# One core, sigmoid attention into routed experts into SwiGLU: table copies on VectorE, ranks first, three block buffers

## The chip, the cores and the metric

The kernel runs on one core of a Trainium2 chip. The metric is the device time of one execution in microseconds. Engines are named as in the profile: PE is TensorE, DVE is VectorE, ACT is ScalarE, POOL is GpSimd, SP is SyncE, which here issues most DMAs. Engines work through their own queues in program order, and wait for each other by semaphores.

## The reference

Three layers stand one behind the other, all in fp32:

```python
# attention: batch 4, 12 heads, 448 positions, head size 64
scores = scale * np.matmul(q, k.transpose(0, 1, 3, 2)) - np.log(S)
attn = 1.0 / (1.0 + np.exp(-scores))
x = np.matmul(attn, v)                         # laid out as 1792 tokens x 768
# experts: 8, inner size 1024, one for each token
logits = x @ w_gate
expert_idx = np.argmax(logits, axis=1)
probs = np.exp(logits - logits.max(-1, keepdims=True))
probs /= probs.sum(-1, keepdims=True) + 1e-09
out[mask] = gate_w[mask, None] * (np.maximum(x[mask] @ w1[e], 0.0) @ w2[e])
# SwiGLU, inner size 1536
g = x @ w_gate2
y = (g / (1.0 + np.exp(-g))) * (x @ w_val) @ w_out
```

## The kernel before

Products of fp32 data are made of three products each: an operand is split into a high part (ACT, for instance `whi`, L1116) and a low part (DVE, `wlo`, L1118), and high by high, low by high and high by low are summed in PSUM. The work goes through four stages.

**Attention, to about 166 us.** 24 units of scores, sigmoid (ACT, `a`, L253) and value products. Beside it, 24 blocks of the last layer's weights, which come as 64-bit numbers, are turned into fp32 by integer steps and stored in DRAM (`wgd`). `load_conv` brings a block (two buffers), `conv_abs` (L482) takes the absolute value of the high words into a tile with tag "w" (on DVE for blocks 0, 1 and the last, otherwise on ACT), `conv_bits` puts the bits together on DVE, and POOL issues the store (L504). The tag "w" has two buffers, so a tile is free again when the store of the block two earlier has landed.

**Routing, about 166 to 188 us.** The gate gives a one-hot `sel` for each token. `ranks` (L364 to L368) counts on PE how many earlier tokens went to the same expert; DVE adds these to `carry` (L378) and computes from them, in a long run of small operations, in which slot and at which row each token stands. `ohh` (L679) is a one-hot of that, `pp` (L694) the product on PE that gives the slot's token list `perm_g`. The gate weight `gw` is one over a sum of exponentials (L682 to L684), cut into three bf16 parts `g3` (L687, L689); `oh` (L710) is the one-hot times these, and `pg` (L714) the product that gives the weights by slot, `gsl`. PE meanwhile makes the first slot's first products (`first_product`, L467, one for each of six blocks), of which number 0 stands ahead of the ranks, 1 to 4 ahead of `pp`, and 5 ahead of `pg`.

**Experts, about 188 to 505 us.** A hand-written order `seq` of 182 products, each with one weight tile: entry (0, s, j) is block j of the first product of slot s, (1, s, j) that of the second. Two steps ahead of a product `split_w` (L1111) splits its weights. `when(kind, s, j, f)` hangs further work on an entry; it is issued after the split for the entry two later and before the entry's own product. Half-filled slots are worked off in the background with unsplit weights, which SP loads into a ring of four tiles (L1256) and PE uses at L1294. The last of these background jobs is one slot shared by two quarter slots of two experts; its table (`duo`, `duo_g`: token, position and gate weight of each of its four groups of `QL` rows) is made by `make_duo` (L1262) with twelve small DMAs on SP at entry 30, each bringing one column from the first `QL` partitions to one of four groups of partitions. Its rows are gathered by POOL at entry 101, and DVE uses its positions at entry 109.

**SwiGLU, from about 505 us.** One level of Strassen's scheme, seven products for eight. The input pieces are made by transposes of the experts' rows (`x_piece`, L915): for the first half during slots 9 to 11, pieces 0, 2, 4 at step 5 and pieces 1, 3, 5 at step 7 of a slot's second product. The PSUM buffers that they use are shared with the transposes of the slots' rows and of their inner activations, whose low parts DVE makes as `xl` and `hl` (L84). In the second stage `at_step(turn, f, d)` hangs work `d` steps behind a named turn. There the blocks 3, 4, 5 (`JO` to `KD-1`) of the output weights are converted as above: `convert_o` spreads eight groups two steps apart (DVE L167, L171, L175, L182, with parts on ACT and POOL), `combine_o` makes sums of them, `store_o` stores those (SP, L1368). They work in a tile `room` that shares its buffer with the sums `ts` (L938) of the second half's inputs. `u` (L1023), `c` (L1029), `m` (L1003) are the sums that DVE makes of PE's results in PSUM.

Of the kernel before, what the change touches and what calls it, by code (L numbers as in the profile page):

```python
# [22 lines left out]
def sigmoid_attention_moe_swiglu_kernel(  # L23
# [18 lines left out]
    P = 128  # L42
# [144 lines left out]
    with ExitStack() as actx:  # L187
# [275 lines left out]
        def first_product(j):  # L463
            if j == 0:
                x0["ps"] = ps_s.tile([P, 2, 512], F32, tag="sc", name="hps0")
            for m in range(2):
                nc.tensor.matmul(x0["ps"][:, m], x0["t"][:, j * P:(j + 1) * P],  # L467
                                 raws[0][j][:, m * 512:(m + 1) * 512],
                                 start=(j == 0), stop=(j == KD - 1))
# [10 lines left out]
            load_r64(conv[i], ("gv"[i // K2], i % K2))  # L480

        def conv_abs(i):  # L482
            cvw[i] = cvp.tile([P, DM], F32, tag="w", name="w", bufs=2)
            hi = conv[i].rearrange("p (n t) -> p n t", t=2)[:, :, 1]
            if i < 2 or i == n - 1:
                nc.vector.tensor_scalar(cvw[i].bitcast(I32), hi, 0x7FFFFFFF, None,
                                        op0=ALU.bitwise_and)
            else:
                nc.scalar.activation(cvw[i], hi.bitcast(F32), AF.Abs)
# [40 lines left out]
        with tc.manual_schedule():  # L530
# [93 lines left out]
            gate(B - 1)  # L624
            ex = rp.tile([CP, T, E], F32, tag="ex", name="ex")
            nc.scalar.activation(ex, sh, AF.Exp)
            first_product(0)
            ranks(B - 1, ps_t.tile([P, 512], F32, tag="tr", name="pr"))()
            first_product(1)

            V = nc.vector
# [11 lines left out]
            places(B - 1)  # L643
            rem = rp.tile([P, 1, E], F32, tag="rem", name="rem")
            V.scalar_tensor_tensor(rem, nti, -float(P), cnt, op0=ALU.mult, op1=ALU.add)
            hq = rp.tile([P, 2, E], F32, tag="hq", name="hq")
            V.tensor_scalar(hq[:, 0:1], rem, float(QL), None, op0=ALU.is_gt)
            V.scalar_tensor_tensor(hq[:, 1:], rem, 0.0, hq[:, 0:1], op0=ALU.is_gt,
# [29 lines left out]
            for i in range(2):  # L678
                V.tensor_tensor(ohh[:, :, i], ohf,  # L679
                                tok2[:CP, i, :, None].to_broadcast(shp), op=ALU.mult)  # L680
            gw = rp.tile([CP, T], F32, tag="gw", name="gw")
            V.tensor_reduce(gw, ex, axis=AX.X, op=ALU.add)  # L682
            V.tensor_scalar(gw, gw, 1e-9, None, op0=ALU.add)
            V.reciprocal(gw, gw)  # L684
            g3 = rp.tile([CP, 3, T], BF16, tag="g3", name="g3")
            for i in range(3):
                V.tensor_copy(g3[:, i], gw)  # L687
                if i < 2:
                    V.tensor_sub(gw, gw, g3[:, i])  # L689
            for j in range(2, KD - 1):  # L690
                first_product(j)
            pp = ps_t.tile([P, 512], F32, tag="tr", name="pp")
# [217 lines left out]
    def x_piece(p, t, j):  # L910
        if p not in rx:
            rx[p] = early.tile([P, 2, 2, K3, TH], F32, tag="rx", name="rx", bufs=1)
        pt = ps_t.tile([P, 512], F32, tag="tr", name="pt")
        for i in range(4):
            nc.tensor.transpose(  # L915
                pt[:, i * TR:(i + 1) * TR],
                rows[p, t, i // 2][:TR, i % 2, j // K3, (j % K3) * P:(j % K3 + 1) * P],
                ident[:TR, :TR])
        x, k, jj = rx[p], j // K3, j % K3
        if t == 1 and k == 0:  # L920
            nc.vector.tensor_sub(x[:, 0, 1, jj], pt[:, :TH], x[:, 0, 0, jj])
            tr[p, 1] = x[:, 0, 1]
        else:
            nc.scalar.copy(x[:, k, t, jj], pt[:, :TH])
# [257 lines left out]
    def when(kind, s, j, f):  # L1182
        at.setdefault((kind, s, j), []).append(f)
# [40 lines left out]
    when(1, 3, 0, lambda: nc.scalar.activation(warm, logs, AF.Sigmoid))  # L1224
    when(0, 9, 0, lambda: load_rows(0, 0))
    for j in range(KD):
        when(1, 9 + j // 2, (5, 7)[j % 2], lambda j=j: x_piece(0, 0, j))
    when(0, L, 0, lambda: load_rows(0, 1))
    for j in range(KD):
        when(1, L - 1, j, lambda j=j: x_piece(0, 1, j))  # L1230
# [25 lines left out]
        nc.sync.dma_start(bgw[n][:, :w], src.rearrange("o p f -> p (o f)"))  # L1256

    def make_duo():
        for i, (t, tbl) in enumerate(((duo[:, 0:1], perm_g), (duo[:, 1:], pos), (duo_g, gsl))):
            for d in range(2):  # L1260
                for h in range(2):
                    nc.sync.dma_start(t[(2 * d + h) * QL:(2 * d + h + 1) * QL],  # L1262
                                      tbl[:QL, NH + d:NH + d + 1])

    def duo_pos():
        nc.vector.tensor_scalar(pos2[:, NH0:], duo[:, 1:], 1, None, op0=ALU.logical_shift_left)
# [64 lines left out]
    for k in range(NH0 + 1):  # L1331
# [5 lines left out]
        ops += [(d, lambda k=k, lo=lo, hi=hi: bg_products(k, lo, hi)) for d, lo, hi in bursts]  # L1337
        for d, f in sorted(ops, key=lambda o: o[0]):
            when(*seq[b0 + d], f)
    when(*seq[30], make_duo)  # L1340
    when(*seq[BG0 + NH0 * BGN], duo_pos)
    when(*seq[BG0 - 4], lambda: [bg_load(n) for n in range(RB)])

# [93 lines left out]
    with tc.manual_schedule():  # L1437
# [245 lines left out]
        for j in range(JO, KD):  # L1683
            if j <= JO + 1:
                key = ((1, 7), (R1 + 1, 5))[j - JO]
                at_step(*key, lambda j=j: next_room(j))
            b0 = ((2, 1), (R1 + 2, 6), (R1 + 2, 6))[j - JO]
            d = 20 * (j == KD - 1)
            for x in range(2):
                for g in range(4):  # L1690
                    at_step(*b0, lambda j=j, x=x, g=g: convert_o(j, x, g), d + 8 * x + 2 * g)
            for h in range(2):
                at_step(*b0, lambda h=h: combine_o(h), d + 15 + 2 * h)
                at_step(*b0, lambda j=j, h=h: store_o(j, h), d + 17 + h)
            if j == JO + 1:
                at_step(*b0, lambda j=j: load_o(j + 1, 0), d + 6)
                at_step(*b0, lambda j=j: load_o(j + 1, 1), d + 14)
# [166 lines left out]
```

## Time and profile before

| | us |
|---|---|
| median of 3 runs | 990.73 (990.13 to 991.36) |
| the profiled execution | 992.88 |
| its span in the trace | 991.1 |
| PE busy | 957.1 |
| DVE busy | 787.4 |
| ACT busy | 587.1 |
| POOL busy | 221.6 |
| mean granted PE clock | 0.995 |
| DMA, mean over the span | 224 GB/s |

The span is what the trace covers; the profiled execution takes a little more than that. "Busy" is the time in which an engine had an instruction running; an engine that is 97% busy can save at most the rest by shorter waits. The page's row of DMA rates by fortieths of the span (24.8 us each) goes up and down between 71 and 367 GB/s until 800 us; the last fortieths, of the output, have little.

### The profile page before, as it was taken

The numbers are of one execution on the slowest core, as the hardware profiler recorded it, in microseconds if no ns is written. First come the engines' busy times: TensorE is split into PE (matmuls) and PEld (weight loads), VectorE is DVE, ScalarE is ACT, GpSimd is POOL, SyncE is SP. The second block draws the span as 40 slices with busy tenths as digits, with TensorE's granted clock in tenths as the row PEclk, the third lists the DMA queues.
The fourth block names the chain that finished last, engine by engine and source line by source line (L and its number), as shares of the span: only waits on it lengthen the run. The fifth ranks groups of instructions, "written<-read, shape, count | busy, mean of one in ns | idle before, by whom it ended". The sixth has DMA issues, their size and how long they took to land. (4 is left out here: it accounts for less than half of the span.)

```text
span 991.1 us, 16157 instructions
## 1 busy us (share of the span) xinstructions
PE 957.1 (97%) x5374; PEld 782.0 (79%) x5374; DVE 787.4 (79%) x1288; ACT 587.1 (59%) x916; POOL 221.6 (22%) x227
## 2 busy tenths in 40 slices
PE   8999999899989999999998999999999999999995
PEld 4555555677667677687888899998999999999995
DVE  7888888988768888777789989898889788966561
ACT  6988883577757677687864444465544545633331
POOL 1000011211120311300147655452122221011101
PEclk9999999999999999999999999999999999999998
DMA  9989979368698676979629575546464867633300
GB/s 332 319 316 344 331 270 367 95 239 303 206 351 276 237 299 194 349 249 357 199 71 299 167 230 165 156 160 235 147 233 144 278 197 267 184 123 102 112 33 32
DMA packets 102906, 222.19 MB, mean 224 GB/s; under 512 B 12288, under 2 KB 59648, under 8 KB 102816
## 3 DMA queue, kind: packets, MB, share of 16 engines
q1 hardware_dynamic: 94448, 188.99, 56.2%
q0 software_dynamic: 6672, 31.09, 8.4%
q10 hardware_dynamic: 1696, 1.02, 0.3%
q8 instruction: 44, 0.72, 0.3%
q14 instruction: 46, 0.38, 0.1%
HBM read 217.49 MB, written 55.46 MB: 275 GB/s over the span
## 5 line engine op out<-in xcount | busy, mean ns | idle before, releaser
L1118 DVE TENSOR_TENSOR wlo<-wraw,whi 128x768 fp32r<-128x768 f32 (+1 forms) x182 | 192.5, 1081 | 63.3 <-ACT whi L1116 55.2
L1116 ACT CAST whi<-wraw 128x768 fp32r<-128x768 f32 (+1 forms) x182 | 167.1, 930 | 81.7 <-PE hps L1165 43.9
L966 PE MATMUL pd<-x,wgh 128*128 128x448 f32 x288 | 82.4, 367 | 1.7 <-DVE c L1029 1.7
L966 PE MATMUL pa<-x,wgh 128*128 128x448 f32 x288 | 82.2, 367 | 0.1
L966 PE MATMUL pc<-x,wgh 128*128 128x448 f32 x288 | 82.4, 367 | 0.0
L857 DVE TENSOR_TENSOR wgl<-sr,wgh 128x384 fp32r<-128x384 f32 x96 | 72.7, 765 | 2.8 <-ACT wgh L854 2.6
L253 ACT ACTIVATE a<-sc,logs 128x896 f32<-128x896 f32 x72 | 68.8, 1005 | 9.4 <-PE sc L261 8.6
L854 ACT CAST wgh<-sr 128x384 fp32r<-128x384 f32 x96 | 48.8, 512 | 38.6 <-PE pd L966 21.8
L1030 POOL TENSOR_TENSOR c<-u,c 128x448 f32<-128x448 f32 x24 | 36.3, 1515 | 154.0 <-DVE c L1029 154.0
L294 PE MATMUL pu<-a,vr 128*64 128x448 f32 x288 | 59.2, 547 | 0.0
L966 PEld LDWEIGHTS pd<-x,wgh 128*128 128x128 f32 x288 | 53.6, 187 | 6.6 <-issue 2.0
L966 PEld LDWEIGHTS pa<-x,wgh 128*128 128x128 f32 x288 | 53.6, 188 | 5.0 <-issue 0.5
L966 PEld LDWEIGHTS pc<-x,wgh 128*128 128x128 f32 x288 | 53.7, 187 | 4.6
L1165 PE MATMUL yps<-whi,hh 128*128 128x384 f32 x208 | 56.7, 353 | 0.0
L1165 PE MATMUL yps<-wlo,hh 128*128 128x384 f32 x208 | 54.1, 341 | 1.8 <-DVE wlo L1118 1.7
L966 PE MATMUL pd<-x,wgl 128*128 128x448 f32 x144 | 52.7, 366 | 0.8 <-DVE wgl L857 0.8
L1165 PE MATMUL yps<-whi,hl 128*128 128x384 f32 x208 | 53.1, 336 | 0.0
L966 PE MATMUL pc<-x,wgl 128*128 128x448 f32 x144 | 52.6, 365 | 0.0
L966 PE MATMUL pa<-x,wgl 128*128 128x448 f32 x144 | 52.4, 364 | 0.0
L1165 PE MATMUL hps<-whi,xh 128*128 128x512 f32 x156 | 51.0, 408 | 0.0
L1165 PE MATMUL hps<-wlo,xh 128*128 128x512 f32 x156 | 49.3, 398 | 1.1 <-DVE wlo L1118 1.1
L1165 PE MATMUL hps<-whi,xl 128*128 128x512 f32 x156 | 48.5, 392 | 0.0
(336 smaller groups left out, 2319.5 us busy)
## 6 DMA issues: line engine op xcount, KB each, us to landing
wraw<-in_moe_w_dram SPq DMA_DIRECT2D x108, 384.0 KB
wraw<-in_moe_w_dram SPq DMA_DIRECT2D x78, 512.0 KB
ring<-in_moe_w_dram SPq DMA_DIRECT2D x30, 512.0 KB
ring<-in_moe_w_dram SPq DMA_DIRECT2D x40, 384.0 KB
w<-wgd SPq DMA_DIRECT2D x36, 384.0 KB
qkr<-in_qkv_dram SPq DMA_DIRECT2D x23, 448.0 KB
hraw<-hd SPq DMA_DIRECT2D x13, 768.0 KB
r<-in_moe_w_gate_dram SPq DMA_DIRECT2D x12, 768.0 KB
```

What stands on the lines that cost most here:

```text
L253: nc.scalar.activation(am[key], sc[:, :, :S], AF.Sigmoid, bias=logs, scale=SCALE)
L294: nc.tensor.matmul(pu[h * D:(h + 1) * D, :S], vt[:, i % 2, c, h], a[:, h], start=False, stop=(c == CK - 1))
L854: nc.scalar.copy(hi, s)
L857: nc.vector.tensor_sub(lo, s, hi.bitcast(F32))
L966: nc.tensor.matmul(ps, st[:, a], mv[:, j], start=(j == 0 and m == 0 and n not in (2, 3, 4)), stop=(j == K3 - 1 and m == 2), skip_group_che ...
L1030: nc.gpsimd.tensor_tensor(t, sb[r, "u"], t, op=ALU.add)
L1116: nc.scalar.copy(hi[:, :w], r)
L1118: nc.vector.tensor_sub(lo[:, :w0], r[:, :w0], hi[:, :w0].bitcast(F32))
L1165: nc.tensor.matmul(ps[:, m, :w], st[:, a], mv[:, m * w:(m + 1) * w], start=(j == 0 and i == 0), stop=(j == m_ - 1 and i == 2))
```

## The change

Five edits.

- `conv_abs`: the tag "w" has three buffers instead of two.
- Routing: the ranks' products go to PE ahead of the first product. The sum of the exponentials is made on POOL as three additions (8 to 4 to 2 to 1) and the small constant, as soon as they are there; the reciprocal stays on DVE, behind `rem` (L645); the three-part cut goes to POOL, five operations.
- `x_piece` of pieces 0, 2, 4: step 6 instead of 5 of the slot's second product.
- `make_duo`: twelve DVE copies instead of twelve DMAs on SP, at `seq` entry 97 instead of 30.
- The conversion of block 3 of the output weights starts six steps later, with all that belongs to it. Blocks 4 and 5 stay.

```diff
-            cvw[i] = cvp.tile([P, DM], F32, tag="w", name="w", bufs=2)
+            cvw[i] = cvp.tile([P, DM], F32, tag="w", name="w", bufs=3)
...
             nc.scalar.activation(ex, sh, AF.Exp)
+            gw = rp.tile([CP, T], F32, tag="gw", name="gw")
+            e4 = rp.tile([CP, T, 4], F32, tag="e4", name="e4")
+            G = nc.gpsimd
+            G.tensor_tensor(e4, ex[:, :, 0:4], ex[:, :, 4:8], op=ALU.add)
+            G.tensor_tensor(e4[:, :, 0:2], e4[:, :, 0:2], e4[:, :, 2:4], op=ALU.add)
+            G.tensor_tensor(gw, e4[:, :, 0], e4[:, :, 1], op=ALU.add)
+            G.tensor_scalar(gw, gw, 1e-9, None, op0=ALU.add)
+            ranks(B - 1, ps_t.tile([P, 512], F32, tag="tr", name="pr"))()
             first_product(0)
-            ranks(B - 1, ps_t.tile([P, 512], F32, tag="tr", name="pr"))()
             first_product(1)
...
             V.scalar_tensor_tensor(rem, nti, -float(P), cnt, op0=ALU.mult, op1=ALU.add)
+            V.reciprocal(gw, gw)
+            g3 = rp.tile([CP, 3, T], BF16, tag="g3", name="g3")
+            for i in range(3):
+                G.tensor_copy(g3[:, i], gw)
+                if i < 2:
+                    G.tensor_sub(gw, gw, g3[:, i])
...
-            gw = rp.tile([CP, T], F32, tag="gw", name="gw")
-            V.tensor_reduce(gw, ex, axis=AX.X, op=ALU.add)
-            V.tensor_scalar(gw, gw, 1e-9, None, op0=ALU.add)
-            V.reciprocal(gw, gw)
-            g3 = rp.tile([CP, 3, T], BF16, tag="g3", name="g3")
-            for i in range(3):
-                V.tensor_copy(g3[:, i], gw)
-                if i < 2:
-                    V.tensor_sub(gw, gw, g3[:, i])
...
-        when(1, 9 + j // 2, (5, 7)[j % 2], lambda j=j: x_piece(0, 0, j))
+        when(1, 9 + j // 2, (6, 7)[j % 2], lambda j=j: x_piece(0, 0, j))
...
     def make_duo():
-        for i, (t, tbl) in enumerate(((duo[:, 0:1], perm_g), (duo[:, 1:], pos), (duo_g, gsl))):
+        for t, tbl in ((duo[:, 0:1], perm_g), (duo[:, 1:], pos), (duo_g, gsl)):
             for d in range(2):
                 for h in range(2):
-                    nc.sync.dma_start(t[(2 * d + h) * QL:(2 * d + h + 1) * QL],
-                                      tbl[:QL, NH + d:NH + d + 1])
+                    nc.vector.tensor_copy(t[(2 * d + h) * QL:(2 * d + h + 1) * QL],
+                                          tbl[:QL, NH + d:NH + d + 1])
...
-    when(*seq[30], make_duo)
+    when(*seq[BG0 + NH0 * BGN - 12], make_duo)
...
-            d = 20 * (j == KD - 1)
+            d = (6, 0, 20)[j - JO]
```

Here `BG0` is 10, `NH0` 3 and `BGN` 33, so the new place of `make_duo` is entry 10 + 99 - 12 = 97.

## Rows read from the trace of the kernel before

**Rows 1.** Page, busy time, share of the span and instructions of each engine.
```profile
PE 957.1 (97%) x5374; PEld 782.0 (79%) x5374; DVE 787.4 (79%) x1288; ACT 587.1 (59%) x916; POOL 221.6 (22%) x227
```

**Rows 2.** Groups by line, PE: count | busy us, mean ns | idle before, releasers.
```profile
L1294 PE MATMUL bps<-ring,xbt 128*64 128x512 f32 (+1 forms) x120 | 25.5, 613 | 4.1 <-DMA ring<-in_moe_w_dram 4.0 <-ACT xbt L1312 0.2
L1294 PE MATMUL bps<-ring,bht 128*64 128x384 f32 (+1 forms) x160 | 23.7, 495 | 1.2 <-DMA ring<-in_moe_w_dram 1.2
...
L915 PE MATMUL pt<-ident,yt 112*128 112x112 f32 x96 | 13.3, 261 | 3.8 <-DVE u L1023 2.2 <-DVE xl L84 1.6
```

**Rows 3.** Timeline of SP (start us, us, engine line op): the shared slot's table DMAs.
```profile
241.49 2.48 SPq L1262 DMA_DIRECT2D duo<-perm_g  x4
...
253.08 1.78 SPq L154 DMA_DIRECT2D wraw<-in_moe_w_dram  x5
```

**Rows 4.** Windows: us, busy PE PEld DVE ACT POOL, PEclk, DMA share, GB/s.
```profile
246.00:256.00 10.00, 9.46 (x50) 7.37 (x46) 9.67 (x11) 6.66 (x7) 0.00 (x0) 1.00 0.05 10
...
284.70:288.10 3.40, 3.40 (x9) 1.82 (x6) 0.00 (x0) 0.00 (x0) 0.00 (x0) 0.50 1.13 393
```

**Rows 5.** Timeline of PE, a ring product of the background [idle before <-releaser].
```profile
283.03 1.08 PE L1294 MATMUL bps<-ring,xbt 128*64 128x512 f32 x4 [2.86 <-DMA ring<-in_moe_w_dram]
```

**Rows 6.** Timeline of DVE and PE, round step 97 and the shared slot's transposes.
```profile
364.69 0.96 DVE L1118 TENSOR_TENSOR wlo<-wraw,whi 128x768 fp32r<-128x768 f32 x1 [0.70 <-ACT whi L1116]
366.69 0.52 PE L1165 MATMUL yps<-wlo,hh 128*128 128x384 f32 x2
384.81 0.82 PE L1273 MATMUL bps<-ident,xg 128*128 128x128 f32 x6
```

**Rows 7.** Timeline of DVE, a small operation of the routing.
```profile
170.69 0.17 DVE L396 TENSOR_SCALAR loi<-posi 112x4 int32<-112x4 int32 x1
```

**Rows 8.** Timeline of DVE, second layer: conversion, sums and the reuse of its tile.
```profile
535.77 0.98 DVE L167 TENSOR_SCALAR room<-room 128x768 int32<-128x768 int32 x1
...
552.04 0.84 DVE L167 TENSOR_SCALAR room<-room 128x768 int32<-128x768 int32 x1
...
554.61 0.61 DVE L1023 TENSOR_TENSOR u<-pb,p 128x448 f32<-128x448 f32 x1
...
575.90 0.63 DVE L1037 TENSOR_TENSOR pc<-pc,u 128x448 f32<-128x448 f32 x1 [1.10 <-PE pc L966]
...
581.83 0.62 DVE L921 TENSOR_TENSOR rx<-pt,rx 128x448 f32<-128x448 f32 x1 [1.62 <-PE pt L915]
...
596.55 0.61 DVE L938 TENSOR_TENSOR ts<-rx 128x448 f32<-128x448 f32 x1
```

**Rows 9.** Timeline of PE, and ACT's semaphore wait at L489 (ns, start).
```profile
24.36 0.47 PE L261 MATMUL sc<-qkh 64*128 64x448 f32 x2 [1.56 <-ACT a L253]
...
L489 ACTq EVENT_SEMAPHORE  x1: 2403/2403/2403, 19.6 to 19.6; - x1
```

**Rows 10.** Timeline of PE and DVE, the routing.
```profile
168.55 0.25 PE L364 MATMUL pr<-sel,ones 112*128 112x8 bf16 x4
169.04 0.17 DVE L378 TENSOR_TENSOR carry<-pr,carry 128x8 f32<-128x8 f32 x1 [1.48 <-PE pr L368]
...
177.37 0.71 PE L694 MATMUL pp<-ohh,ohl 112*128 112x68 bf16 x16 [1.39 <-DVE ohh L679]
...
178.96 1.99 DVE L710 TENSOR_TENSOR oh<-ohf,g 112x544 bf16<-112x544 bf16 x3
...
181.00 0.92 PE L714 MATMUL pg<-oh,ohl 112*128 112x102 bf16 x16 [1.13 <-DVE oh L710]
```

**Rows 11.** Timeline of POOL and DVE: a small operation, and two engines together.
```profile
147.04 0.29 POOL L415 TENSOR_TENSOR before<-rot 128x64 f32<-128x64 f32 x1
...
552.42 1.32 POOL L831 TENSOR_TENSOR sr<-w,sr 128x384 f32<-128x384 f32 x1
552.80 1.35 DVE L857 TENSOR_TENSOR wgl<-sr,wgh 128x384 fp32r<-128x384 f32 x1
...
555.14 0.54 DVE L857 TENSOR_TENSOR wgl<-w,wgh 128x384 fp32r<-128x384 f32 x1
```

## The prediction

> **What bounds the kernel now.** I read the page's busy times first: TensorE (PE) is busy 957.1 of 991.1 us [rows 1], so the rest matters only where PE stands still, 34 us at most. Second, the PE groups by line, for what ended PE's waits [rows 2]: products with ring weights waited 4.0 and 1.2 us on DMA, and the transposes of L915 waited 2.2 on `u` and three times together 1.6 on `xl`, both VectorE's (DVE). Third, the timeline round each place, for what runs ahead of the work that PE awaits. A part of the change is worth what it takes from such a wait and no more: DVE has idle time in most stages.
>
> **The shared slot's columns.** The twelve DMAs hold SP's queue from 241.49 until the next weight loads go out at 253.08, 11.6 us [rows 3]. In 246 to 256 DMA runs at a share of 0.05 and 10 GB/s [rows 4], though PE consumes weights as before. Then PE waits for ring loads: 1.2 us in the second-product group [rows 2] and 2.86 at 283.03 [rows 5], after which its clock is granted at 0.50 for 3.4 us [rows 4], half of it lost: 1.7. Together 1.2 + 2.9 + 1.7 = 5.8. The other ring waits of the first-product group, 4.0 - 2.9 = 1.1, I leave standing. With the DMAs gone, SP issues those loads 11 us sooner into a stretch with hardly any traffic, so I take the waits as caused by the hole.
>
> The twelve copies come on DVE at step 97, behind one `wlo` and ahead of the next. No row shows a copy that shifts partitions; the nearest is a small op of four columns, 0.17 us [rows 7], so 12 x 0.17 = 2.0. Cover: DVE idles 0.70 before `wlo` at 364.69, which ends at 365.65 and is used at 366.69, 1.04 later [rows 6]; so 1.7 is hidden and 0.3 shows. If the copies overlap, nothing shows; a price of 0.5 each would show 4.3. The gather from `duo`, on POOL, has to follow the copies and so comes at about 365 at the soonest; behind it on that queue stand other slots' gathers and stores, which the same order puts several products ahead of their readers. PE reads the gathered rows at 384.81 [rows 6], 20 us after. Net **-5.5**, bounds -6 to 0 (a DMA wait that stays).
>
> **Pieces of the Strassen input one step later.** The three even pieces wait for a PSUM buffer that DVE's `xl` frees, 1.6 together [rows 2]. One step later a product of six matmuls stands in front; two take 0.52 [rows 6], so over 1 us against waits of 0.53. DVE reads the buffer by then, and PE's own work fills the time. ACT's copy of the piece moves with it, behind the next `whi`. **-1.6**, bounds -1.6 to +0.5 (ACT late by one cast).
>
> **One conversion six steps later.** From 535.77 to 552.04 five conversion instructions stand in DVE's queue ahead of `u` at 554.61, the first of 0.98, the last of 0.84 [rows 8]; `u` ends PE's wait of 2.2 [rows 2]. Starting six steps later, at two steps a group, three of the five stand behind `u`: 3 x 0.9 = 2.7 > 2.2, so the wait goes. The moved work falls where DVE idles 1.10 before 575.90 and 1.62 before 581.83 [rows 8]: 2.7 against three ops of 0.98 or less and two sums. Its ACT and POOL parts move along. Its stores go six steps later too: eight steps took 552.04 - 535.77 = 16.3, so six are 12 us. The tile that they read is wanted again by `ts` at 596.55 [rows 8]; the stores' place, step 31 or about 16 x 2.03 = 32.5 after 535.77, is 568 and becomes 580, so 16 us to land. **-2.0**, bounds -2.2 to +0.5 (a moved op just ahead of something PE awaits).
>
> **Third buffer.** PE waits 1.56 for `a` at 24.36; ACT had stood ahead of L489, in `conv_abs`, from 19.6 for 2.4 us [rows 9]. At that point the two `w` buffers hold blocks 0 and 1, whose stores on POOL had just been issued, so the new tile waits for one to land; a third needs none. ACT is then early by 2.4, more than 1.56. The later waits of this kind I count at nothing, because no PE wait of note follows one. **-1.5**, bounds -1.56 to 0 (the wait is for the block's load instead).
>
> **Ranks first, sums on POOL.** DVE waits 1.48 for ranks, which PE starts at 168.55 behind the first product; `carry` starts at 169.04 [rows 10]. So `sel` was ready at 167.56, and ranks first gives `carry` at 167.60 + 0.49 = 168.09, 0.95 sooner. DVE's chain to `ohh` keeps its length plus the reciprocal, 0.2, so `ohh` is ready at 177.37 - 0.95 + 0.21 = 176.63. PE: from 167.60 the ranks and products up to `pp` take what they took from 168.55 to 175.98 (177.37 less the wait of 1.39) plus the product once ahead, about 1.8 (2.50 less the 0.71 of `pp`, below): 167.60 + 7.43 + 1.8 = 176.8. `pg` came 181.00 - 1.13 - 177.37 = 2.50 behind `pp` without its own wait, so 179.3. Its operand `oh` takes 1.99, ready 178.6 if the weight sums, which stood between 177.32 and 178.96, are gone. So `pg` starts at 179.3 instead of 181.00, 1.7 sooner, and all behind it shifts.
> POOL's side: small ops there take 0.29 [rows 11]. Four sums from the exponentials are 1.2 us, while DVE has 14 instructions from `carry` to the reciprocal, 14 x 0.17 = 2.4; the five ops of the three-part split take 1.5 and are needed only 5 us later. Neither is waited for. What may bite is DVE being held while POOL works. At 552.80 `wgl` takes 1.35 with POOL's `sr` running from 552.42 for 1.32; at 555.14, free of it, an equal one takes 0.54 [rows 11]. Nine POOL ops of 0.29 could hold the chain by 2.6: then `ohh` is at 179.2 and `pg` at 181.7, 0.7 later than now. DVE ops that read PSUM or one operand are many in that chain, so I take a loss of 0.3. **-1.4**, bounds -1.7 to +0.7.
> The Trainium skill, in "SBUF — State Buffer", section "Who interferes with whom", has this as a rule: a DVE op with two SBUF inputs and a GpSimd op that reads SBUF share one port pair, held for a whole instruction. The rows on `wgl` agree (1.35 against 0.54). By it alone, with every POOL op falling on a two-input op, this part would be the +0.7 just worked out; by the rows without contention it is -1.7.
>
> **Sum.** 5.5 + 1.6 + 2.0 + 1.5 + 1.4 = 12.0. The span becomes 979.1; the profiled run took 992.88, 1.8 more than its span, and becomes 980.9. It lay 2.15 above the median, 990.73, so the median becomes **978.7**.
>
> **Rivals.**
> (a) The ring waits stay. DMA has work enough elsewhere, so loads issued sooner may only wait for the transfers ahead of them; the clock's fall says only that PE stood. For it: from 284.70 DMA shows no room, 1.13 [rows 4]. Against: a stretch of 10 us with next to no traffic lies just ahead, and with the ring loads issued before it there is time in it for them. Then 5.5 is lost: 984.2. Chance 0.08.
> (b) DVE is what comes late. POOL holds it during routing (+0.7 instead of -1.4: 2.1 lost), and the moved conversion stands ahead of the input pieces' sums near 581 (the 2.0 returns). Either gives 980.7 to 980.8, both 982.8. For it: the stretched `wgl` [rows 11], and DVE's full queue up to 555. Against: its idle 2.7 us at the new place [rows 8]. Chance 0.14.
> (c) Slower: the copies. Should a copy into other partitions cost p, they hold 12p of DVE's queue ahead of a `wlo`, of which 1.7 is covered. The change breaks even when 12p - 1.7 passes what the rest gains, 12.0 + 0.3, so at p = 1.2; with p = 1.5 it is 978.7 + 16.3 - 0.3 = 994.7, and 996.4 with a clock fall like that of [rows 4]. For it: no row shows such a copy. Against: every tiny DVE op here takes a sixth of that [rows 7]. Chance 0.05, of which 0.02 near no change.
> (d) The third buffer does not do what it says: ACT waits for the block's load, which is issued late whatever the buffers. 980.2. For it: the wait's row doesn't name its releaser. Against: the load is issued two blocks ahead. Chance 0.03.
>
> **How the numbers follow.** My forecast has 0.70, so 978.7. Its own spread, by the bounds of the parts that may come fully or with small losses, is 977 to 981. The range takes in (a) and (b), so up to 985, and down to 976.5, if all parts reach their full worth (5.8 + 1.6 + 2.2 + 1.56 + 1.7 = 12.9: 977.8) and smaller waits shorten with them. That leaves out about 0.1. About 0.2%, 2 us, is what a measurement here can tell from no change: faster covers all cases but (c), 0.95; same 0.02; slower 0.03.
>
> **What would show it.** In the profile after: no DMA on SP between 241 and 253 but weight loads, GB/s in 246 to 256 in the hundreds, no PE wait above 1 us on the ring, and no granted clock of 0.50 behind one. Twelve copies near 363, of 0.2 us or less, with no PE wait on `wlo` behind them. L915's waits of 3.8 under 1 in all. ACT's first wait in `conv_abs` gone and PE's gap of 1.56 near 23 with it. PE waiting once, about 1 us, for `sel` ahead of the ranks, and `pg` right behind the last product. Wrong would be: a new DMA wait of 1 us or more in 250 to 300 [(a)], new DVE waits of PE at 176 to 181 or 575 to 590 [(b)], copies over 0.5 us each [(c)], or ACT still waiting near 19.6 [(d)].

## The result, and the profile after

The changed kernel takes 982.55 us (median of 6 runs, 980.63 to 987.09) beside 991.32 us (6 runs, 990.13 to 992.82) for the kernel before: the ratio is 0.9915 with a 95% interval of 0.9892 to 0.9938, so 8.8 us faster by the medians and 6.1 to 10.7 by the interval. The forecast was 978.7 us, that is 12.0 us less, with a range of 976.5 to 985.0. The direction and the range held; some 3 us of the gain are missing. The profiled execution of the changed kernel took 983.25 us with a span of 981.5.

Read the page first, as before: busy time by engine, share of the span, instructions.

```profile
PE 955.3 (97%) x5374; PEld 782.5 (80%) x5374; DVE 790.7 (81%) x1293; ACT 586.2 (60%) x916; POOL 223.9 (23%) x236
```

PE has the same 5374 matmuls as in [rows 1] and still sets the time. The groups by line answer to [rows 2] (the change adds four lines above, so L1294 is now L1298, L915 is L919); columns are count, busy us, mean ns, idle before, releasers.

```profile
L1298 PE MATMUL bps<-ring,xbt 128*64 128x512 f32 (+1 forms) x120 | 25.7, 610 | 2.3 <-DMA ring<-in_moe_w_dram 2.1 <-ACT xbt L1316 0.2
L1298 PE MATMUL bps<-ring,bht 128*64 128x384 f32 (+1 forms) x160 | 23.5, 494 | 0.0
...
L919 PE MATMUL pt<-ident,yt 112*128 112x112 f32 x96 | 13.3, 260 | 2.5 <-DVE u L1027 1.6 <-DVE rx L925 0.9
```

The 1.2 of the second-product group is gone, the 1.6 on `xl` too. But 2.1 us on the ring stay, the wait on `u` fell from 2.2 to 1.6 only, and there is a new wait of 0.9 on `rx`. The next rows are PE's timeline round the ring wait (beside [rows 5]) and three windows, the last of the stretch behind the wait (us, busy PE PEld DVE ACT POOL, granted clock, DMA share, GB/s).

```profile
276.25 1.08 PE L1298 MATMUL bps<-ring,xbt 128*64 128x512 f32 x4 [1.52 <-DMA ring<-in_moe_w_dram]
...
242.00:252.00 10.00, 9.46 (x50) 7.37 (x46) 9.67 (x11) 6.65 (x7) 0.00 (x0) 1.00 0.46 155
250.00:255.00 5.00, 5.00 (x28) 3.36 (x28) 4.39 (x5) 2.11 (x2) 0.00 (x0) 1.00 0.00 0
...
278.10:281.40 3.30, 3.30 (x10) 1.92 (x7) 0.00 (x0) 0.00 (x0) 0.00 (x0) 0.50 1.05 407
```

The wait is 1.52 instead of 2.86, and the clock falls to 0.50 (its lower level) behind it as before. The hole of [rows 4] is gone all the same. PE is 4.0 us earlier here, so the stretch of its work that lay at 246 to 256 lies at 242 to 252 now (50 matmuls and 9.46 us of PE in both), and DMA moves 155 GB/s in it instead of 10. A shorter hole stands behind it, 250 to 255, with no traffic. In it SP issues weight loads that move nothing: `load_w` takes a condition (`cond=nv[s + 1]`), and where the next slot has the same expert its weights are there already.

Why the wait stays although its hole is filled, SP's and PE's rows tell, of the kernel before and then of the changed one (start, us, engine, line):

```profile
255.11 1.86 SPq L1256 DMA_DIRECT2D ring<-in_moe_w_dram  x3
...
273.40 1.26 SPq L1256 DMA_DIRECT2D ring<-in_moe_w_dram  x3
...
279.10 1.08 PE L1294 MATMUL bps<-ring,xbt 128*64 128x512 f32 x4
```

```profile
243.63 2.00 SPq L1260 DMA_DIRECT2D ring<-in_moe_w_dram  x3
...
267.74 1.49 SPq L1260 DMA_DIRECT2D ring<-in_moe_w_dram  x3
...
273.65 1.08 PE L1298 MATMUL bps<-ring,xbt 128*64 128x512 f32 x4
```

The three ring loads that SP had held back, at 255.11, go out at 243.63; the first of them is the one whose lateness made PE wait 1.2. The loads that PE waits for in the burst at 279.10 are others, those of 273.40. `bg_products` issues them behind the burst ahead of that one (at 269.10, and at 263.67 in the changed kernel), for the tiles which it has used, so they could not go out in the hole: 5.7 us ahead of their own burst in the kernel before, 5.9 in the changed one.

### The profile page after: what moved, and what is told of

The parts are those of the page before. It is cut to its first block, busy times and chain, and to the rows that moved or that the text cites. A ratio compares the mean times of both kernels' runs of the same rounds, so it can differ in the third digit from the quotient of the medians.

```text
span 981.5 us, 16167 instructions
## 1 busy us (share of the span) xinstructions
PE 955.3 (97%) x5374; PEld 782.5 (80%) x5374; DVE 790.7 (81%) x1293; ACT 586.2 (60%) x916; POOL 223.9 (23%) x236
## 3 DMA queue, kind: packets, MB, share of 16 engines
q10 hardware_dynamic: 1696, 1.02, 0.4%
```

## Experiments

Each kernel is the changed one with one edit, unless it says otherwise. Where a place is compared, it is by the start of the same instruction in two traces.

**The changed kernel again**, for what differs between executions of one program.

> The changed kernel as it is, once more. Two theories of what made it 982.55 us where 978.7 was forecast, apart from the ring. Theory P: in the second layer a matmul of 448 columns starts either 200 or 207 ns after the one before, for long stretches, and the pace changes only where PE has paused; which one follows a pause is not fixed by the program. Then this profile has other slow stretches than the first one (117 us of the 280 us of such products at 207 ns, from about 558 to 669 us), and the time moves with them by 0.033 us for each us of slow stretch, some 3 us either way. Theory Q: the pace belongs to the place in the program (its buffers, its DMAs), and the same stretch, 558 to 669, is at 207 ns again. Both expect the ring wait near 274.7 at about 1.5 us again, a granted clock of 0.50 for 3.4 us right behind it, the wait on u near 544.7 at about 1.6 and the one on rx near 574.8 at about 0.9.

Measured: 983.8 us (4 runs, 978.87 to 985.6), ratio 0.9921 (0.9903 to 0.9939). The profiled execution was the fastest, 978.87 with a span of 977.1, 4.4 us below the first profile of the same program. Of that, 0.24 is the ring wait (1.28 for 1.52), 1.7 the clock, which did not fall, 0.6 the wait on `u` (1.08 for 1.64) and 1.8 the pace: from 505 us on the matmuls of 448 columns start mostly 200 ns apart, where the first profile had them mostly 207 ns apart from about 558 to 668. Theory P holds in that the pace is not fixed by the program; that it changes only where PE has paused does not hold (last section). This is how it looks in the timeline of two executions of the kernel *before*, its first profile and `e12_before_again` (below), in the same place:

```profile
705.45 0.37 PE L966 MATMUL pc<-x,wgl 128*128 128x448 f32 x1
705.66 0.57 PE L966 MATMUL pc<-x,wgh 128*128 128x448 f32 x2
706.07 0.37 PE L966 MATMUL pc<-x,wgl 128*128 128x448 f32 x1
```

```profile
705.30 0.36 PE L966 MATMUL pc<-x,wgl 128*128 128x448 f32 x1
705.50 0.56 PE L966 MATMUL pc<-x,wgh 128*128 128x448 f32 x2
705.90 0.36 PE L966 MATMUL pc<-x,wgl 128*128 128x448 f32 x1
```

Three matmuls take 0.62 us in one and 0.60 in the other, with no idle time, the same instructions, and a granted clock of 1.00 in both.

**The conversion back at its old place.**

```diff
-            d = (6, 0, 20)[j - JO]
+            d = (0, 0, 20)[j - JO]
```

> The changed kernel with one edit undone: the conversion of block 3 starts at its old place, six steps earlier. Theory of the prediction: the move is worth 2.0 us, so this kernel is 2 us slower, with a wait on u of 2.2 us near 544. Rival: DVE has caught up with PE at the sum that it makes some 8 us ahead of u, so only conversion instructions behind that point delay u; in both kernels two of them stand there (1.7 and 1.8 us of DVE time), and the move takes only 0.5 off the wait and adds 0.9 of waiting on rx near 575, where its two sums stand. By the rival this kernel is 0.2 to 0.6 us faster where the pace is equal: the wait on u is 2.0 to 2.3, the wait on rx is gone.

Measured: 983.45 us (4 runs, 980.51 to 984.97), ratio 0.9916 (0.99 to 0.9933), not to be told from the changed kernel. Its profile and that of `e1_again` have the same pace from 506 us on, so the traces can be set side by side: at the `u` transposes this kernel is 1.0 us further behind than before them (wait 2.08 against 1.08), and at the `rx` transposes it has that 1.0 back, since it doesn't wait there. The move is worth 0.0 us in this pair. L919 in this kernel, then in `e1_again`:

```profile
L919 PE MATMUL pt<-ident,yt 112*128 112x112 f32 x96 | 13.2, 260 | 2.1 <-DVE u L1027 2.1
```

```profile
L919 PE MATMUL pt<-ident,yt 112*128 112x112 f32 x96 | 13.3, 260 | 1.9 <-DVE u L1027 1.1 <-DVE rx L925 0.9
```

**Most of that conversion left out.**

```diff
-                for g in range(4):
+                for g in range(4 if j > JO else 1):
```

> The changed kernel with six of the eight groups of the conversion of block 3 left out (the output weights of that block are then not right): only the first group of each half stays, with its loads, sums and stores. If DVE's conversion work is what makes u late, the wait on u near 544.7 falls from 1.64 by the 1.3 us of the one group that is left out ahead of it, to 0.3 or less; the wait on rx near 575 falls from 0.91 to nothing only if DVE's backlog there comes from the groups and not from the two sums, which stay. If u is late for another reason (PE's own product, POOL's), the wait stays at 1.6.

Measured: 978.92 us (one run). L919 waits for nothing any more:

```profile
L919 PE MATMUL pt<-ident,yt 112*128 112x112 f32 x96 | 13.2, 259 | 0.0
```

So the conversion's groups cause both waits, the one on `rx` as well, though the two sums are still there: the sums alone do not delay it. That part of the mechanism was right; the place was not. The groups' parts on ACT and POOL are left out too, so that it is DVE's share that counts is argued, not shown.

**The background burst one entry later.**

```diff
-    halves = ((2, 3, 12, 15, 16, 32),
-              ((5, 0, 3), (11, 3, 6), (18, 6, 9), (25, 9, 12), (31, 12, 14)))
+    halves = ((2, 3, 13, 15, 16, 32),
+              ((5, 0, 3), (12, 3, 6), (18, 6, 9), (25, 9, 12), (31, 12, 14)))
```

> The changed kernel with the second burst of background products of each half slot one entry of the order later (12 instead of 11, and its relu 13 instead of 12). Theory R: the ring wait of 1.52 us near 274.7 is left because the loads are issued only 6 us before their use, behind four weight loads on SP, while a load takes 8.5 us to land with DMA full; one product in between gives PE 1.4 us or more of other work, so the wait falls to 0.3 or less and the clock does not fall behind it: 1.5 + 0.2 + 1.7 = 3.4 us gained where the pace is equal. Theory S: DMA is full and PE only meets the same lack of data a little later, at the next weight tile or at the next burst; then a wait of 1 us or more comes back between 276 and 300 and the gain is under 1 us. If the clock falls at the same place without a wait ahead of it, the fall is not the wait's.

Measured: 980.85 us (4 runs, 980.07 to 981.74), ratio 0.9885 (0.9868 to 0.9901). The wait near 275 is gone, and comes back at the next burst:

```profile
287.16 0.87 PE L1298 MATMUL bps<-ring,bht 128*64 128x384 f32 x4
288.70 0.87 PE L1298 MATMUL bps<-ring,bht 128*64 128x384 f32 x4 [0.68 <-DMA ring<-in_moe_w_dram]
290.67 0.90 PE L1298 MATMUL bps<-ring,bht 128*64 128x384 f32 x4 [1.10 <-DMA ring<-in_moe_w_dram]
```

0.68 + 1.10 = 1.8 us there, and the clock fell behind these. Theory S: PE met the same lack of data later. By place, PE was 1.4 us behind `e1_again` at 294. The median lies 3 us lower than that of `e1_again` (983.8), and the intervals of the two ratios just miss each other; but one of the four runs of `e1_again`, 978.87, is below all four here, and the place that was edited does not explain a gain.

**The copies alone, in the kernel before** (`make_duo` as in the change, nothing else).

> The kernel before with the shared slot's twelve copies alone (on DVE at entry 97 in place of the DMAs at 30). Theory of the prediction: SP's hold of 11.6 us causes both large ring waits; all of 5.8 us goes, less 0.3 for the copies, so 985 to 986. Rival: only the first wait (1.2 near 257) is SP's; the second, 2.86 near 280, is shortened by 1 to 1.5 and stays, because DMA is full from 256 on whatever SP does before, with the clock's fall behind it or not; then 2.2 to 3 us are gained without the fall's end, 4.5 with it, the median 987 to 989. Both expect copies of 0.16 us start to start and no PE wait on wlo at that place, and that the three waits of 0.53 on xl and the wait on u of 2.2 are as before.

Measured: 990.26 us (10 runs, 987.68 to 993.37) beside 993.26, ratio 0.9961 (0.9942 to 0.9979): 3.9 us, 2.1 to 5.8 (the medians are 3.0 apart). In its profile:

```profile
L1294 PE MATMUL bps<-ring,xbt 128*64 128x512 f32 (+1 forms) x120 | 25.3, 602 | 3.0 <-DMA ring<-in_moe_w_dram 1.7 <-issue 1.1 <-ACT xbt L1312 0.2
L1294 PE MATMUL bps<-ring,bht 128*64 128x384 f32 (+1 forms) x160 | 23.5, 494 | 0.0
L915 PE MATMUL pt<-ident,yt 112*128 112x112 f32 x96 | 13.7, 266 | 4.5 <-DVE u L1023 2.9 <-DVE xl L84 1.6
```

The 1.2 is gone; ahead of 281.09 and 283.29 PE waits 0.81 and 1.12. Beside the first profile of the kernel before that is 2.3 us less of waits. The clock did not fall here, but in two other places of this execution. Over all runs it fell less: the mean granted clock is 0.9944 in the ten runs with the copies and 0.9925 in the 13 without. A fall of 3.4 us to 0.50 lowers that mean by 0.0017 and costs 1.7 us, so the difference is worth about 1.9 us (an estimate). About half of what the copies gain is clock, then.

**Two buffers again.**

```diff
-            cvw[i] = cvp.tile([P, DM], F32, tag="w", name="w", bufs=3)
+            cvw[i] = cvp.tile([P, DM], F32, tag="w", name="w", bufs=2)
```

> The changed kernel with two buffers for the tag w again. The prediction has the third buffer worth 1.5 us, all of it at the gap near 22.8; the later waits at nothing. Then the gap of 1.56 is back, and PE reaches the first instruction of the ranks 1.5 to 1.6 us later than in the changed kernel. Rival from the trace after: the shift between the two kernels was 2.2 us by 165.6, so the waits on later stores cost PE another 0.6 (at the end of attention, where DVE had waited 2.31 us for a store's landing); then the ranks come 2.1 to 2.3 later. If the block's load were what ACT waits for, neither would come back.

Measured: 983.19 us (one run). The gap is back at 1.53 (beside 1.56 in [rows 9]), and ACT's wait too; PE starts the ranks at 167.50 beside 165.61 in `e1_again`, 1.9 us later:

```profile
24.36 0.47 PE L261 MATMUL sc<-qkh 64*128 64x448 f32 x2 [1.53 <-ACT a L253]
...
167.50 0.26 PE L364 MATMUL pr<-sel,ones 112*128 112x8 bf16 x4 [1.22 <-DVE sel L357]
```

ACT's row at that place in the changed kernel:

```profile
19.65 0.91 ACT L489 ACTIVATE w<-r 128x768 f32<-128x768 f32 x1 [1.08 <-DMA r<-in_moe_w_gate_dram]
```

Between the two expectations, 1.5 to 1.6 and 2.1 to 2.3. The buffer is what ACT waits for with two. In the changed kernel it still waits 1.08, now for the block's load, and goes on at 19.65, ahead of PE's need.

**The gate weight's sums back on DVE, the ranks still first** (the eight DVE operations behind `ohh`, as before).

> The changed kernel with the gate weight's sums and the cut in three back on DVE behind ohh, and the ranks still ahead of the first product. By the prediction's working the weight sums stand 1.6 us between ohh and oh, so pg waits for oh again: ohh ends 0.25 earlier without the reciprocal, oh starts 1.6 later, and pg starts 1.3 us later than in the changed kernel, with a PE wait of 1.3 on oh ahead of it. If POOL's work holds DVE there, DVE's chain from carry to the end of ohh is shorter without it by more than the reciprocal's 0.2, up to 2.6 us; in the trace after it took 8.3, as before.

Measured: 986.82 us (one run; 6.0 of them in a PE wait at 403.8 that no other kernel here had, behind ACT, which waits 8.0 us for an earlier store of the experts' rows; why that store is late stays open). In the routing:

```profile
172.87 1.36 DVE L679 TENSOR_TENSOR ohh<-ohf,tok 112x544 bf16<-112x544 bf16 x2
...
175.88 1.99 DVE L710 TENSOR_TENSOR oh<-ohf,g 112x544 bf16<-112x544 bf16 x3
...
177.92 0.92 PE L714 MATMUL pg<-oh,ohl 112*128 112x102 bf16 x16 [0.98 <-DVE oh L710]
```

`pg` waits 0.98 for `oh`. From the transposes of the first slot to `pg` are 15.35 us in the kernel before, 14.53 here and 13.39 in the changed kernel: 0.8 of this part's gain is the ranks' place, 1.1 the sums'. From `carry` at 165.95 to the end of `ohh` at 174.23 are 8.28 us without POOL beside it.

**The input pieces at step 5 again.**

```diff
-        when(1, 9 + j // 2, (6, 7)[j % 2], lambda j=j: x_piece(0, 0, j))
+        when(1, 9 + j // 2, (5, 7)[j % 2], lambda j=j: x_piece(0, 0, j))
```

> The changed kernel with the pieces 0, 2, 4 of the Strassen input at step 5 again. The prediction has the move worth 1.6 us: three PE waits of 0.53 on xl at L919 come back, between 417 and 464 us, and PE is 1.6 us later behind the third. Rival from the alignment of the two traces: each place gained about 1.0, more than its wait, because PE's first product behind the pause runs apart from the weight loads; then PE is 2.5 to 3 us later behind the third. A second rival, that ACT's copies behind the next cast give part back: less than 1.2 us.

Measured: 984.95 us (one run). The three waits are back, one of them in the first lines here; the next two lines are the same place in `e1_again`.

```profile
417.38 0.51 PE L1169 MATMUL yps<-whi,hl 128*128 128x384 f32 x2
418.42 0.57 PE L919 MATMUL pt<-ident,yt 112*128 112x112 f32 x4 [0.53 <-DVE xl L84]
```

```profile
415.91 0.51 PE L1169 MATMUL yps<-whi,hl 128*128 128x384 f32 x2
416.26 0.55 PE L919 MATMUL pt<-ident,yt 112*128 112x112 f32 x4
```

From the pair of products to the transposes 1.04 us pass with the wait and 0.35 without: 0.69, not the 0.53 that stands as idle. A matmul of 0.34 us is overlapped by the next, which starts 0.17 behind it; a pause lays the other 0.16 bare. Three times that is 2.1 us, and by place this kernel is 2.0 further behind `e1_again` at 500 us than at 416. That is more than the prediction's 1.6 and less than the first rival's 2.5 to 3, whose reason it bears out; ACT's copies give nothing back.

**The stores of the converted blocks earlier.**

```diff
-            when(*seq[spots[c + 4] + 2 * h], lambda j=j, h=h: store_o(j, h))
+            when(*seq[(spots[c + 3] + 3, spots[c + 4])[h]], lambda j=j, h=h: store_o(j, h))
```

> The changed kernel, with the stores of the output weights' blocks 0 to 2 in the expert stage earlier: the first half (0.79 MB) three entries of the order after its sums (entry 38 instead of 41 for block 0), the second half (0.59 MB) at entry 41 instead of 43. DVE's order stays. Theory R: the ring wait near 274.7 (1.3 to 2.2 us in the kernels run so far) is left because DMA is full from 256 to 281 and the ring loads queue behind what was issued before; from 251 to 256 it moves only some 30 GB/s, because the next slot's weights are the ones that are there and their loads are skipped. Then 0.79 MB moved from 255 to about 250 takes 0.79 MB / 0.39 MB per us = 2.0 us out of the queue ahead of the ring loads, and the wait falls to 0.3 or less, with no fall of the clock behind it. Rival S: the ring loads' lateness is SP's own, which issues them at 267.7 behind four weight loads; a store moved ahead changes nothing, the wait stays at 1.3 or more.

Measured: 983.52 us (5 runs, 981.92 to 985.29), ratio 0.991 (0.988 to 0.9939). The window of 251 to 256 in the changed kernel's first profile and here, and the ring wait:

```profile
251.00:256.00 5.00, 5.00 (x29) 3.37 (x28) 3.39 (x5) 1.84 (x3) 0.00 (x0) 1.00 0.18 36
251.00:256.00 5.00, 5.00 (x29) 3.37 (x28) 3.53 (x5) 1.84 (x3) 0.00 (x0) 1.00 0.61 194
```

```profile
275.40 2.21 PE L1298 MATMUL bps<-ring,xbt 128*64 128x512 f32 x8 [0.53 <-DMA ring<-in_moe_w_dram]
```

194 GB/s where there were 36, and a wait of 0.53, where nine profiles with this burst and the copies, but with the stores at their old place, have 1.5 to 2.6 in all; the clock did not fall. SP issued the ring loads at 267.88, as in `e1_again` (267.84). That speaks for the queue of data and against SP, but it is one execution: `e11_both` (below) has the same stores, 188 GB/s in that window and its ring loads at 267.80, and waits 1.43 in all. The time doesn't show a gain. The profiled execution had the matmuls from 583 to 815 mostly at 207 ns and lost 4.5 us to `e1_again` there; the pace of the other runs is not known.

**The conversion in denser steps.**

```diff
-                    at_step(*b0, lambda j=j, x=x, g=g: convert_o(j, x, g), d + 8 * x + 2 * g)
+                    at_step(*b0, lambda j=j, x=x, g=g: convert_o(j, x, g),
+                            d + (8 * x + 2 * g if j > JO else 4 + 4 * x + g))
+            e = d if j > JO else d - 2
             for h in range(2):
-                at_step(*b0, lambda h=h: combine_o(h), d + 15 + 2 * h)
-                at_step(*b0, lambda j=j, h=h: store_o(j, h), d + 17 + h)
+                at_step(*b0, lambda h=h: combine_o(h), e + 15 + 2 * h)
+                at_step(*b0, lambda j=j, h=h: store_o(j, h), e + 17 + h)
```

> The changed kernel with the eight groups of block 3's conversion one step apart instead of two, from four steps later (steps 10 to 17 of the hook's count instead of 6 to 20), and its sums and stores two steps earlier (19 and 21 instead of 21 and 23). Theory T: what delays u near 543 is the two conversion instructions that stand behind the point where DVE has caught up with PE, 1.8 us of DVE time; here none stands there, so the wait on u (1.0 to 1.6 in the changed kernel) goes, and the sums stand ahead of the input pieces, so the wait on rx (0.9) goes as well: 2 us gained where the pace is equal. Rival U: DVE has no room for eight groups of 0.9 to 1.4 us in eight steps of 2 us each beside its own 75 to 90%; its backlog then delays u or c of the next turn, and waits of 1 us or more come up between 548 and 572; the gain is nothing or less.

Measured: 980.75 us (4 runs, 980.05 to 982.92), ratio 0.9879 (0.9845 to 0.9912). The wait on `u` is gone, as theory T has it; the one on `rx` grew to 1.7 instead of going, and ahead of it stands a sum of 2.13 us (two operations, from 572.61). By place, against `e1_again`, 1.3 was gained at `u` and 0.8 lost at `rx`.

**Both of these together.**

> The changed kernel with the two edits that each took waits away: the stores of the output weights' first blocks earlier, and block 3's conversion in steps one apart. If the two add up, the ring wait near 275 is 0.6 us or less, the wait on u is gone and the one on rx is 1.7 at most: 1.0 + 0.6 us better than the changed kernel at equal pace and without the clock's fall, 1.7 more where that kernel's clock falls; a median of 980 to 981.5 against 983. If the pace of the second layer's matmuls outweighs them, its runs spread over 978 to 986 like those of the changed kernel and the medians can't be told apart.

Measured: 980.0 us (6 runs, 979.11 to 982.24) beside 991.41, ratio 0.9877 (0.985 to 0.9905). This is the lowest median of several runs here, 11.4 us under the kernel before. The waits that are left:

```profile
L1298 PE MATMUL bps<-ring,xbt 128*64 128x512 f32 (+1 forms) x120 | 25.3, 603 | 2.4 <-DMA ring<-in_moe_w_dram 2.2 <-ACT xbt L1316 0.2
...
L919 PE MATMUL pt<-ident,yt 112*128 112x112 f32 x96 | 13.2, 260 | 1.0 <-DVE rx L925 1.0
```

The ring's 2.2 here are 1.22 + 0.21 near 275 and others of 0.5 or less. The 0.6 that was expected near 275 did not come: of the two profiles with the earlier stores one has 0.53, the other 1.43, just under the 1.5 to 2.6 without them. Against the changed kernel the interval of the ratio still overlaps (0.9892 to 0.9938), so that it beats it is likely and not shown.

**The kernel before again.**

> The kernel before, once more. Two profiles with its second layer (its own and that with the copies alone) had the matmuls of 676 to 826 us at 207 ns, all 526 of them; of the ten profiles with the changed second layer or its variants two had much of that stretch at 207. Theory V: the pace of that stretch belongs to the old order of the second layer, and this profile has it at 207 again: then 5 us of the change's gain are pace. Theory P: it is drawn anew in each execution, whatever the kernel, and 200 is as likely.

Measured: 989.82 us (one run). Its matmuls from 522 us on start mostly 200 ns apart, also those of 676 to 826: theory P. Of the profiles with the changed second layer only `e9_store_early` had that stretch slow, not two. Against the first profile of the same kernel this one gains 2.8 us from 676 to 815, not the 5 that was expected, because a slow stretch has some starts at 200 and a fast one some at 207 (means of 205.4 and 201.3 ns from 700 to 720). It waited 2.05 us at 22.9, and its clock fell to 0.50 behind that, not behind the 1.78 us near 282. With 0.23 behind it that ring wait is 2.0 us, where the first profile had 3.06: it lies within the 1.5 to 2.6 of the kernels with the copies.

## Why the prediction was right in direction and 3 us too large

By its own steps:

- **The copies' price** was right. Twelve of them take 1.92 us, three rows of four (start, us, engine, line, tiles), and the `wlo` behind them makes PE wait for nothing:

```profile
357.11 0.61 DVE L1266 COPY duo<-perm_g 32x1 int32<-32x1 int32 x4
357.75 0.62 DVE L1266 COPY duo<-pos 32x1 int32<-32x1 int32 x4
358.38 0.62 DVE L1266 COPY duog<-gsl 32x1 f32<-32x1 f32 x4
359.03 0.96 DVE L1122 TENSOR_TENSOR wlo<-wraw,whi 128x768 fp32r<-128x768 f32 x1
```

  Rival (c) is out: 0.16 us each for copies that shift partitions.
- **The ring: forecast 5.5 with the clock; in waits 2.3 to 2.5 beside the first profile of the kernel before** (1.2, and 2.86 + 0.20 against 1.52 + 0.23 or 0.81 + 1.12), **1.4 to 1.6 beside its second** (1.11 + 1.78 + 0.23 against 1.52 + 0.23 or 1.28 + 0.21). The failed step is "SP issues those loads 11 us sooner", and with it "I take the waits as caused by the hole". For the wait of 1.2 both hold: its loads went out at 243.63 instead of 255.11, and no kernel with the copies has that wait. For that of 2.86 they do not: its loads go out behind PE's burst at 269.10, long after the hole, 5.9 us ahead of their use instead of 5.7. The hole was SP's, and filling it left this wait where it was. Its length differs between executions (2.0 and 3.1 before, 1.5 to 2.6 with the copies), so that anything was gained at this place is not shown. Rival (a), which had 0.08, had the outcome for this wait, though not the reason: these loads were not issued sooner.
- **The clock: 1.7, counted as gained with that wait.** It is not tied to it: it fell behind it in the changed kernel's first profile and not in its second. But over many runs the size was about right. The mean granted clock is 0.9928 in 39 runs of the kernel before (those beside the experiments) and 0.9954 in ten of the changed kernel, which, worked out as under the copies alone, is an estimate of 2.6 us of the span; the copies alone had 1.9. The cause that the prediction gave for its 1.7 was wrong, and that the number fits is luck.
- **The pieces: forecast 1.6, measured 2.1**, because a pause costs 0.16 us more than its idle time, as worked out under the input pieces at step 5.
- **The conversion: forecast 2.0, measured 0.0.** The failed step is that three of the five instructions ahead of `u`, moved behind it, take 2.7 us off its wait. DVE's timeline in the changed kernel:

```profile
537.13 0.63 DVE L1041 TENSOR_TENSOR pc<-pc,u 128x448 f32<-128x448 f32 x1 [1.02 <-PE pc L970]
...
538.20 0.55 DVE L167 TENSOR_SCALAR room<-room 128x768 int32<-128x768 int32 x1
...
541.78 1.37 DVE L171 SCALAR_TENSOR_TENSOR room<-room 128x768 int32<-128x768 int32 x1
...
545.72 0.61 DVE L1027 TENSOR_TENSOR u<-pb,p 128x448 f32<-128x448 f32 x1
...
571.00 0.97 DVE L1366 TENSOR_TENSOR room<-room 128x384 f32<-128x384 f32 x1
```

  With three instructions fewer in front, DVE reaches `pc` early and waits 1.02 us there for PE. What was taken out ahead of that point came back mostly as idle time. Behind it two conversion instructions stand ahead of `u`, 0.46 + 1.30 = 1.8 us from start to start; in the kernel with the old place there are two as well, of 0.87 + 0.74 = 1.6. And at the new place the groups and the two sums behind them delay `rx`: the loss that the prediction gave as its bound of +0.5, and that rival (b) had with 0.14, is 0.9. The idle time of 1.10 and 1.62 that I counted as cover [rows 8] is used up: in the changed kernel DVE runs without a gap from 567 to 580. The 0.0 is one pair of profiles. Over all of them the waits on `u` and `rx` together are 2.1 to 2.9 with the old place (four profiles, 2.5 on average) and 1.0 to 2.7 with the new one (seven, 2.0), so some 0.5 may have been gained, and 2.0 was not.
- **The third buffer: forecast 1.5, measured 1.9.** The gap of 1.56 went, and most of the rest came with it: `e6_two_buffers` loses 1.6 to `e1_again` at the gap's first matmul and 0.2 more by 25.3 us. That the later waits are worth about nothing was right. ACT's first wait is not gone, as the prediction had it: 1.08 of it stays, for the block's load, and PE does not feel it. Rival (d) is out.
- **The routing: forecast 1.4, measured 2.0** (`pg` at 181.00 before and 176.87 after, 4.13, less 2.17 that were gained by the transposes of the first slot at 165.65 and 163.48). The bound of -1.7 was nearer than the value taken. The chain that carried the argument, in the changed kernel:

```profile
166.05 0.17 DVE L378 TENSOR_TENSOR carry<-pr,carry 128x8 f32<-128x8 f32 x1 [0.56 <-PE pr L368]
...
173.00 1.36 DVE L692 TENSOR_TENSOR ohh<-ohf,tok 112x544 bf16<-112x544 bf16 x2
...
174.53 0.70 PE L698 MATMUL pp<-ohh,ohl 112*128 112x68 bf16 x16
...
176.87 0.92 PE L718 MATMUL pg<-oh,ohl 112*128 112x102 bf16 x16
```

  `pp` and `pg` wait for nothing, and `carry` to the end of `ohh` is 8.31 us with nine POOL operations beside it, 8.28 before and in `e7_sums_dve`. So POOL's small operations did not hold DVE here, and the 0.3 that I took off was not needed. Nor was that for want of overlap. All nine run between 166.59 and 170.27, and a DVE operation with two inputs beside one of them takes 0.29, as it does in `e7_sums_dve` without:

```profile
169.08 0.29 DVE L664 TENSOR_TENSOR t<-before,hq 128x128 f32<-128x128 f32 x1
169.12 0.33 POOL L658 TENSOR_TENSOR gw<-gw,g 112x16 f32<-112x16 f32 x1
```

  The Trainium skill's rule on the shared port pair ("SBUF — State Buffer", "Who interferes with whom") agrees with `wgl` in [rows 11], and no DVE operation of this chain shows it.

Measured parts: 2.5 + 2.1 + 0.0 + 1.9 + 2.0 = 8.5, beside 8.8 for the whole. The forecast's 12.0 had 3.0 too much for the ring and its clock, 2.0 for the conversion, and 0.5 + 0.4 + 0.6 too little elsewhere: 12.0 - 5.0 + 1.5 = 8.5. That 8.5 comes so near to 8.8 is in part luck: the 2.5 is the larger of the values for the ring, the clock's 2.6 is not in the sum, and the pace, which differed by up to 4.5 us between executions, is known of the profiled ones alone.

## What to carry to other kernels

A hole in the DMA traffic just ahead of a wait need not be its cause: find the loads that the wait is for, and ask whether they could have been issued in the hole at all. Here they could not, and the wait stayed when the hole was filled. Compare windows of two kernels by the work that lies in them, not by their times, and see whether conditional loads move bytes. Of work that is moved out of an engine's queue, only what stands behind the last point where that engine waits for its data counted here; ahead of that point the time turned into idle time. And a pause of PE costs its idle time plus the overlap that a running stream would have had, here 0.53 + 0.16.

## What the runs showed of the hardware

- **Two paces of the same matmuls.** In the second layer a stream of 448-column matmuls starts mostly every 200 or mostly every 207 ns, at a granted clock of 1.00 both times, for up to 230 us on end. One program had different paces in two executions: the kernel before was slow from 676 to 826 in its first profile and fast there in the second, the changed kernel slow from about 558 to 668 in its first and fast there in its second. In the 14 profiles the pace mostly changed where waits or transposes break the stream, but not always: in the changed kernel's first profile three matmuls take 0.62 us up to 526.07 and 0.60 from 527.28 on, with no wait and no transposes between. Such a slow stretch costs about 2%: 2.8 us of 139, 4.5 of 232. That is more than any one part of this change. With the clock it is a likely reason why the runs of the changed kernel spread from 978.9 to 987.1, of which two are profiled. What decides the pace stays open.
- **The clock's fall behind a wait is not fixed by its length.** For 3.4 us each it fell to 0.50 behind PE waits of 1.52, 1.72, 2.05, 2.22, 2.40, 2.86 and 2.90 us, and behind two of 0.68 and 1.10 with 0.87 us of work between; it did not behind others of 1.28, 1.53, 1.58, 1.90, 2.08, 2.19 and 2.92, nor behind two of 0.81 and 1.12.
